# Three squares, a store's sum, four first products and the last column halves change places in a one-core attention and feed-forward kernel

## The chip, the cores and the metric

The kernel runs on one core of a Trainium2 chip. The metric is the device time of one execution in microseconds (us). Five executions of the kernel before are given; their median is 208.82 us. One more view of it is a profile: one execution recorded by the hardware, with the start and duration of every instruction, its span, and the landing of every transfer.

## What is computed

The reference has two steps. The first is a cross attention of tokens `x` (8 batches, 8 heads, 512 tokens, 64 columns) and 32 `state` rows per head, in both directions:

```
scores  = x @ state^T / 8          xread = softmax(scores)  @ state
scores2 = state @ x^T / 8          sread = softmax(scores2) @ x
a_out   = concat([xread, sread])   # 544 rows per head
```

The second takes the 8 batches x 544 rows of `a_out`, with the heads side by side as 512 columns, as tokens of a feed-forward layer with 2048 hidden units:

```
h = a_out @ w_in                   # 512 -> 2048
g = s * relu(h)^2 + b
out = g @ w_out                    # 2048 -> 512
```

`s` and `b` are scalars. The output has 4352 rows of 512 fp32 values.

## The kernel before, in words

**Stages of a batch.** For the 512 token rows of a batch, the kernel does not form `xread`. It multiplies the state with `w_in` first: `M` = state times `w_in` (`att_M`, four pieces of 512 hidden units, products into PSUM and a copy to SBUF), and then the hidden layer is `h = a4 @ M`, where `a4` are the softmax shares. The scores `T` (`att_T`) need `x` transposed (`xT`) and the state transposed (`stT`). For batches 0 and 1, `x` is transposed on TensorE (`att_xT_pe`), in two groups `g` of two PSUM tiles each, and the tiles are copied to SBUF, the second tile of a group by ScalarE, the first by VectorE; for later batches a DMA transposes. An exponential on ScalarE gives `E`. For batches 0 to 2 the shares come from sums by TensorE (`att_D`) with Ln and Exp on ScalarE and a product on VectorE; for batches 3 to 7 VectorE forms them in transposed layout (`att_shares`, tile `aT`) and a DMA transposes them into `a4` (`att_a4_dma`, line 307). `att_V` forms the read of the state rows, whose tokens of all batches are worked on at the end as "sr".

**Hidden layer.** `mm1_x(b, f)` forms 128 hidden units `f` (16 of them) of all 512 tokens with two products of 512 columns into a bank `h`. `mm1_close` takes the ReLU (ScalarE, for batch 0 and f = 1, 3, 5 VectorE) into a tile `r` of two `f`, in a pool of three buffers, and after every odd `f` squares the pair into `g` (line 428, VectorE). For batch 0 the squares of f = 1 and 3 are put into a list `held`, and worked off when the square of f = 5 comes.

**Second layer.** Most of it is done by a scheme with 7 block products instead of 8 (`fast_items`): p = 1 to 7, each over 8 blocks k of the hidden units, on sums of token blocks (`token_sum`, VectorE) and of weight blocks (`weight_sums`). Three accumulators in PSUM, A, B and C, carry partial sums from one p to the next; after each p, VectorE takes a sum out (`done`, `put`, `put_last`), and stores go out. A tile in PSUM that VectorE reads is written again only when it has been read. "0b" is the second half of batch 0's tokens, in this scheme with one block of 128 tokens instead of two; the first half of batch 0 goes straight (`mm2_part`, accumulators `o`). For batch 7, accumulator C is two tiles of 256 columns, `oC_0` and `oC_1`, in the pool `psO`; its last product, p = 3, is done for the second of them in two column halves of 128, the second of which begins when VectorE has read the first.

**Order of the work.** TensorE, SP and GpSimd run in the order in which the program is written; for VectorE and ScalarE a scheduler orders the instructions, and `tc.issue_after(i)` puts an instruction behind `i`. Within a batch s, the loop at line 953 runs over f; around each `mm1_x(s, f)` it puts the stages of batch s + 1 (`pieces`) and a slice `items[f]` of seven second-layer products, of batch s - 1 at first and of batch s in the last slices. For batches 2 to 6 the slice comes ahead of `mm1_x` where 4 <= f < 13, and behind it elsewhere (line 956). After batch 7 come the state rows and the rest of batch 7's second layer, in the order of the calls of `go` (lines 1014 to 1025).

Of the kernel before, what the change touches and what calls it, by code (L numbers as in the profile page):

```python
# [9 lines left out]
FP32 = mybir.dt.float32  # L10
# [4 lines left out]
def kernel(  # L15
# [10 lines left out]
    nc = tc.nc  # L26
    AF = mybir.ActivationFunctionType
    ALU = mybir.AluOpType
# [6 lines left out]
    P = 128  # L35
# [10 lines left out]
    NDT = 3  # L46
    NH = DM // 2
# [15 lines left out]
    psH = ctx.enter_context(tc.tile_pool(name="psH", bufs=2, space=bass.MemoryType.PSUM))  # L63
# [5 lines left out]
    def mm(out, lhsT, rhs, start=True, stop=True, tp=None, is_transpose=None):  # L69
        return nc.tensor.matmul(  # L70
            out,
            lhsT,
            rhs,
            start=start,
            stop=stop,
            tile_position=tp,
            is_transpose=is_transpose,
            skip_group_check=True,
        )
# [21 lines left out]
    s_bc = konst.tile([P, 1], FP32, name="s_bc")  # L101
# [75 lines left out]
    xT_done = {}  # L177
# [226 lines left out]

    held = []

    def mm1_close(key, hps, ntok, f):
        if f % 2 == 0:
            pool, tag, n = (apool, "ET", 3) if (key, f) == (0, 0) else (rpool, "r", 3)
            R2[key] = pool.tile([P, 2, ntok], FP16, name=f"r_{key}_{f}", tag=tag, bufs=n)  # L410
        r16 = R2[key]
        if key == 0 and f in (1, 3, 5):
            nc.vector.tensor_scalar(r16[:, f % 2], hps, 0.0, None, ALU.max)
            G["last"] = nc.cur_bb.bb.instructions[-1]
        else:
            nc.scalar.activation(r16[:, f % 2], hps, AF.Relu)  # L416
            G["relu"] = nc.cur_bb.bb.instructions[-1]
        if f % 4 == 0:
            G4[key, f // 4] = gpool.tile([P, 4, ntok], FP16, name=f"g_{key}_{f}", tag="g")
        gt = G4[key, f // 4]  # L420
        G[key, f] = gt[:, f % 4]
        if key == 1 and f in (3, 5):
            with tc.issue_after(nc.cur_bb.bb.instructions[-1]):
                nc.scalar.square(gt[:, f % 4 - 1 : f % 4 + 1], r16)
        elif f % 2 == 1:

            def square():
                nc.vector.tensor_mul(gt[:, f % 4 - 1 : f % 4 + 1], r16, r16)  # L428

            if key == 0 and f in (1, 3):  # L430
                held.append(square)
                return
            while held:
                with tc.issue_after(G["last"]):
                    held.pop(0)()
                G["last"] = nc.cur_bb.bb.instructions[-1]
            square()
            G["last"] = nc.cur_bb.bb.instructions[-1]

# [44 lines left out]
    def x_dst(b, rr):  # L484
        return out_BSn[b, 0:S].rearrange("(q c) n -> c q n", c=SCH)[chunk_of(rr)]
# [64 lines left out]
    def fast_items(b):  # L550
# [11 lines left out]
        def lhs(p, k, i):  # L562
            c = P * i
            a = c0 + c
            if p == 1:
                return G[key, k][:, a : a + P]
            if p == 2:
                return G[key, 8 + k][:, a : a + P]
            if p == 4:
                return G[key, 8 + k][:, th + a : th + a + P]  # L570
            si = {3: 4, 5: 1, 6: 2, 7: 3}[p]
            return SQ[b, si, k // 4][:, k % 4, c : c + P]

        def rhs(p, k):
            if p == 1:
                return wof(k)[:, 0:NH]
            if p == 2:
                return wof(8 + k)[:, 0:NH]
            if p == 3:
                return wof(8 + k)[:, NH:DM]  # L580
            ti = {4: 3, 5: 0, 6: 1, 7: 2}[p]
            return wd[ti][k // 4][:, k % 4, :]
# [9 lines left out]
        def put(bank, add, j, n0):  # L592
            if b == "sr":
                ends.append(own[1][:, len(ends) : len(ends) + 1])
                osb = ends[-1]
            elif j == 1:
                osb = add
            else:
                osb = opool.tile([P, ni, NH], FP32, name=f"osb_{b}_{j}_{n0}", tag="osb")
            if bank == "C" and b == last_b:  # L600
                for i in range(ni):
                    nc.vector.scalar_tensor_tensor(
                        osb[:, i], acc["C", i], s_bc, add[:, i], ALU.mult, ALU.add
                    )
            else:
                nc.vector.scalar_tensor_tensor(osb, acc[bank], s_bc, add, ALU.mult, ALU.add)
            if b == "sr":
                for i in range(4):
                    dst = out_BSn[4 * j + i, S:ST, n0 : n0 + NH]
                    eng = nc.sync if i % 2 else nc.scalar  # L610
                    eng.dma_start(dst, osb[Ns * i : Ns * i + Ns, 0])
                return
            if b == "0b":
                nc.gpsimd.dma_start(x_dst(0, 2 + j)[:, n0 : n0 + NH], osb[:, 0])
                return
            dst = out_BSn[b, 0:S].rearrange("(q ci cj) n -> cj q ci n", ci=2, cj=2)
            nc.gpsimd.dma_start(dst[j][:, :, n0 : n0 + NH], osb)  # L617

        def put_last(i, w=slice(0, NH)):
            ends.append(spare(f"osb_last_{len(ends)}"))  # L620
            osb = ends[-1][:, i, w]
            nc.vector.scalar_tensor_tensor(  # L622
                osb, acc["C", i][:, w], s_bc, kept["u2"][:, i, w], ALU.mult, ALU.add
            )
            dst = out_BSn[b, 0:S].rearrange("(q ci cj) n -> cj ci q n", ci=2, cj=2)
            dst = dst[0][i][:, NH:DM][:, w]
            if len(ends) == 1:
                nc.scalar.dma_start(dst, osb)
            elif len(ends) == 2:
                nc.sync.dma_start(dst, osb)  # L630
            else:
                for eng, p in ((nc.sync, 0), (nc.scalar, P // 2)):
                    eng.dma_start(dst[p : p + P // 2], osb[p : p + P // 2])
# [28 lines left out]
        def item(p, k, i, h=None):  # L662
            bank = {1: "A", 2: "A", 6: "B", 7: "B", 4: "B", 5: "C", 3: "C"}[p]
            fresh = p in (1, 6, 5) and k == 0
            if bank == "C" and b == last_b:
                if fresh:
                    acc[bank, i] = psO.tile([P, NH], FP32, tag="o", name=f"oC_{b}_{i}")
                dst = acc[bank, i]
            else:
                fresh = fresh and i == 0  # L670
                if fresh:
                    pool, tag = psO, "o"
                    if b == "sr":
                        pool, tag = (psH, "h") if bank == "C" else (psA, "att")
                    acc[bank] = pool.tile([P, ni, NH], FP32, tag=tag, name=f"o{bank}_{b}")
                dst = acc[bank][:, i, :]
            if h is not None:
                w = slice(P * h, P * h + P)
                mm(dst[:, w], lhs(p, k, i), rhs(p, k)[:, w], start=False, stop=(k == 7))
                if k == 7:  # L680
                    put_last(i, w)
                return
            mm(dst, lhs(p, k, i), rhs(p, k), start=fresh, stop=(k == 7))
            if p == 3 and b == last_b:
                if k == 7:
                    put_last(i)
            elif k == 7 and i == ni - 1:
                done(p)

# [6 lines left out]
            order = [(p, 0, 8) for p in (1, 6, 2, 7, 5, 4, 3)]  # L696
        out = [(p, k, i) for p, k0, k1 in order for k in range(k0, k1) for i in range(ni)]
        if b == last_b:
            out += [(5, k, i) for i in range(ni) for k in range(8)]
            out += [(3, k, 0) for k in range(8)]  # L700
            out += [(3, k, 1, h) for h in range(2) for k in range(8)]
        return [lambda a=a: item(*a) for a in out]

    def bias_sum():
# [53 lines left out]
    with tc.manual_schedule(engines={ET.PE, ET.SP, ET.Pool}):  # L758
# [67 lines left out]
        with tc.issue_after(A[0]["exp"]):  # L826
# [5 lines left out]
        warm_up(2)  # L832
        mm1_x4(0, 0, lambda: att_M(0, 1, "split"))

        b0 = {
            4: [lambda: att_M(0, 2, "split")],
            9: [lambda: att_xT_pe(1, 0), lambda: att_xT_pe(1, 1)],
            10: [lambda: att_T(1, [0, 1])],
            11: [
                lambda: att_M(0, 3, "split"),  # L840
# [95 lines left out]
        for s in range(1, B):  # L936
# [16 lines left out]
            for f in range(NKF):  # L953
                for fn in todo_s.get((f, "ahead"), []):
                    fn()
                if 1 < s < last_b and 4 <= f < 13:
                    for fn in items[f]:
                        fn()
                    items[f] = []
# [28 lines left out]
                    late_sum = sums.pop()  # L988
                for fn in items[f]:
                    fn()  # L990
                if s == 1 and f == 8:
                    with tc.issue_after(G["u2", "0b"]):
                        sums.pop(0)()
                    sums.append(late_sum)
# [7 lines left out]
        def go(items, n):  # L1002
            for _ in range(n):
                items.pop(0)()
# [15 lines left out]
                token_sum("sr", i, 1)  # L1020
        go(rest, 8)
        go(rows, 4)
        go(rest, 8)
        go(rows, 44)
        go(rest, len(rest))

# [28 lines left out]
```

## Time and profile before

| what | value |
|---|---|
| five executions, us | 208.69, 208.74, 208.82, 209.57, 209.67 |
| median, us | 208.82 |
| profiled execution, us | 209.57 |
| its span, us | 207.8 |
| TensorE matmul busy, share of the span | 198.3 us, 95% |
| VectorE busy | 166.1 us, 80% |
| ScalarE busy | 127.8 us, 62% |
| GpSimd busy | 38.8 us, 19% |
| bytes moved by DMA | 25.52 MB, mean 123 GB/s |
| TensorE clock granted | full, in all slices |

How to read the rows that follow. PE is TensorE's matmul side, PEld its weight loads, DVE is VectorE, ACT ScalarE, POOL GpSimd, SP the queue of SyncE. A row of the order of time gives the start in us, the busy time in us, engine, line, operation, output and inputs by the program's names, how many instructions are merged (x16), and in brackets how long the engine stood idle before them and what ended that. Matmuls are pipelined: the row of a matmul ends when its last result is out, while the next can start much earlier. A row of a wait gives who waited for whom, the total in us, how often, and the longest. "h", "oA", "oB", "oC", "T", "D" and "Mps" are PSUM tiles of the stages above; line 70 is the helper that issues every matmul.

### The profile page before, as it was taken

What the parts mean: (1) busy time and instruction counts of PE and PEld (TensorE: products, weight loads), DVE (VectorE), ACT (ScalarE), POOL (GpSimd) and SP (SyncE); (2) the same over time, 40 slices, a digit from 0 to 9 for tenths busy, and PEclk for the clock granted to TensorE, in tenths of its full rate; (3) what the DMA queues carried; (4) which work ended last, traced back from release to release, by engine and by line L of the source; (5) the groups of instructions that cost most, each with busy time, mean ns of one, the idle gap of its engine ahead of it and who ended that gap; (6) DMA issues with size and microseconds to landing.
All of it is one profiled execution on the core that took longest, in us unless ns stands there. A gap on an engine that the chain in (4) does not pass through costs nothing.

```text
span 207.8 us, 4884 instructions
## 1 busy us (share of the span) xinstructions
PE 198.3 (95%) x1978; PEld 133.1 (64%) x1978; DVE 166.1 (80%) x300; ACT 127.8 (62%) x253; POOL 38.8 (19%) x66
## 2 busy tenths in 40 slices
PE   7888999999999999999999899999999999999991
PEld 2424343566766776767666667676767777888891
DVE  4489679987969996899679966997699786796861
ACT  2578876899477657766676568675867545543100
POOL 5870002413210231023102101120112012100210
PEclk9999999999999999999999999999999999999999
DMA  5999996999999495939891924160416011300243
GB/s 170 229 201 206 207 192 102 183 196 160 138 193 180 117 182 73 201 87 205 126 101 56 194 66 104 50 161 0 101 54 158 3 50 50 106 0 2 89 129 90
DMA packets 46795, 25.52 MB, mean 123 GB/s; under 512 B 31604, under 2 KB 44788, under 8 KB 46772
## 3 DMA queue, kind: packets, MB, share of 16 engines
q0 software_dynamic: 15568, 16.19, 40.0%
q1 hardware_dynamic: 30324, 8.52, 25.3%
q10 hardware_dynamic: 880, 0.49, 0.9%
q8 instruction: 15, 0.25, 0.5%
q14 instruction: 8, 0.07, 0.1%
HBM read 17.30 MB, written 8.91 MB: 126 GB/s over the span
## 4 chain that ended last, share of the span: by engine, by line
PE 85%; DVE 5%; DMA 4%; ACT 3%; issue 1%; POOL 0%; DVEq 0%
PE h L70 24%; PE oB L70 18%; PE oC L70 12%; PE oA L70 11%; PE Mps L70 4%; PE o L70 3%; PE h_sr L70 3%; DMA a<-aT 2%; DMA stf<-in_state_dram 2%; DVE g L428 2%; PE V L70 1%; PE oB_sr L70 1%; PE T L70 1%; ACT r L416 1%; DVE M L337 1%
## 5 line engine op out<-in xcount | busy, mean ns | idle before, releaser
L416 ACT ACTIVATE r<-h 128x512 f16<-128x512 f32 x125 | 73.9, 602 | 44.9 <-PE h L70 44.3
L70 PE MATMUL h<-a,M 128*128 128x512 f16 x256 | 74.1, 379 | 1.1 <-DMA a<-aT 0.6
L70 PEld LDWEIGHTS <-s 128*128 128x128 f16 x456 | 44.0, 98 | 16.3 <-issue 0.6
L428 DVE TENSOR_TENSOR g<-r 128x1024 f16<-128x1024 f16 x62 | 42.0, 683 | 13.6 <-ACT r L416 13.1
L70 PEld LDWEIGHTS <-g 128*128 128x128 f16 x392 | 37.3, 98 | 18.5 <-issue 4.4
L70 PE MATMUL oB<-wd,s 128*128 128x256 f16 x224 | 32.8, 273 | 0.0
L70 PE MATMUL oA<-wo,g 128*128 128x256 f16 x224 | 32.5, 273 | 0.0
L70 PEld LDWEIGHTS <-M 128*128 128x128 f16 x256 | 24.4, 98 | 11.6 <-issue 2.2
L617 POOL DMA_DIRECT2D out_dram<-osb x13 | 8.8, 674 | 70.5 <-DVE rt L352 36.2
L314 ACT CAST M<-Mps 128x1024 f16<-128x1024 f32 x20 | 20.1, 1007 | 0.0
L70 PE MATMUL oC<-wd,s 128*128 128x256 f16 x112 | 16.5, 273 | 0.0
L70 PE MATMUL oC<-wo,s 128*128 128x256 f16 (+1 forms) x120 | 15.5, 265 | 0.4 <-DVE osb_last L622 0.4
L70 PE MATMUL oB<-wd,g 128*128 128x256 f16 x112 | 15.7, 273 | 0.0
L617 POOL DMA_DIRECT2D out_dram<-u x7 | 4.7, 678 | 41.7 <-DVE inv L297 27.5
L416 ACT ACTIVATE r_sr<-h_sr 128x256 f16<-128x256 f32 x16 | 6.1, 382 | 7.9 <-PE h_sr L70 6.4
L644 DVE SCALAR_TENSOR_TENSOR u<-oB,s_bc,qa 128x512 f32<-128x512 f32 x7 | 5.2, 750 | 6.4 <-PE oB L70 6.2
L238 ACT ACTIVATE E<-T 128x256 f16<-128x256 f32 x20 | 7.4, 383 | 4.0 <-PE T L70 4.0
L546 DVE TENSOR_TENSOR s<-s,g 128x1024 f16<-128x1024 f16 x14 | 9.6, 687 | 0.2
L70 PE MATMUL h_sr<-srdT,wi 128*128 128x256 f16 x64 | 9.6, 273 | 0.0
L548 DVE TENSOR_TENSOR s<-g,s 128x1024 f16<-128x1024 f16 x14 | 9.6, 685 | 0.0
L544 DVE TENSOR_TENSOR s<-g,g 128x1024 f16<-128x1024 f16 x14 | 9.6, 684 | 0.0
L539 DVE TENSOR_TENSOR s<-g 128x1024 f16<-128x1024 f16 x14 | 9.5, 686 | 0.0
(137 smaller groups left out, 242.3 us busy)
## 6 DMA issues: line engine op xcount, KB each, us to landing
out_dram<-osb POOLq DMA_DIRECT2D x15, 256.0 KB, 4.4
xn<-in_x_dram POOLq DMA_DIRECT2D x7, 512.0 KB, 9.4
wi<-in_moe_w_in_dram POOLq DMA_DIRECT2D x4, 512.0 KB, 9.0
wo<-in_moe_w_out_dram POOLq DMA_DIRECT2D x4, 512.0 KB, 16.1
out_dram<-u POOLq DMA_DIRECT2D x7, 256.0 KB, 2.5
out_dram<-qb POOLq DMA_DIRECT2D x7, 256.0 KB, 3.2
xf<-in_x_dram SPq DMA_DIRECT2D x2, 512.0 KB, 5.2
out_dram<-osb_0b POOLq DMA_DIRECT2D x2, 128.0 KB, 6.4
```

Of the source, the lines that this page charges most:

```text
L70: return nc.tensor.matmul(out, lhsT, rhs, start=start, stop=stop, tile_position=tp, is_transpose=is_transpose, skip_group_check=True,)
L238: nc.scalar.activation(a["E"][:, g, 256 * m : 256 * m + 256], Ts[m][:, g, :], AF.Exp, scale=scale, accum_out=a["rs"][:, NG * m + g : NG * ...
L314: nc.scalar.copy(dst, ps)
L337: nc.vector.tensor_copy(dst[:, 0], two[0])
L416: nc.scalar.activation(r16[:, f % 2], hps, AF.Relu)
L428: nc.vector.tensor_mul(gt[:, f % 4 - 1 : f % 4 + 1], r16, r16)
L539: nc.vector.tensor_sub(o, a11, a21)
L544: nc.vector.tensor_add(o, a21, a22)
L546: nc.vector.tensor_sub(o, SQ[b, 1, j], a11)
L548: nc.vector.tensor_sub(o, a12, SQ[b, 2, j])
L617: nc.gpsimd.dma_start(dst[j][:, :, n0 : n0 + NH], osb)
L644: nc.vector.scalar_tensor_tensor(u, acc["B"], s_bc, kept["qa"], ALU.mult, ALU.add)
```

## The change

Four places are changed.

1. In batch 0 the squares of f = 1, 3, 7 and 9 are held. The square of f = 3 is released ahead of that of f = 5. Those of f = 1, 7 and 9 are released behind VectorE's last copy of batch 1's transposed tokens.
2. The square of batch 1, f = 11, is held and put behind the sum that is taken out of oC of "0b" in that step.
3. For batches 3 to 6 (`NDT` is 3), the slice of seven products of f = 0 comes ahead of the first products of the hidden layer.
4. For batch 7 the second tile of accumulator C is two tiles of 128 columns, the first in the pool `psO`, the second in `psH`, in product p = 5 already; p = 5 of this tile is thus 16 products of 128 columns where it was 8 of 256, and the sum behind it is two instructions.

```diff
+    def release(i, n):
+        for _ in range(n):
+            with tc.issue_after(G["last"]):
+                held.pop(i)()
+            G["last"] = nc.cur_bb.bb.instructions[-1]
...
-            if key == 0 and f in (1, 3):
+            if (key, f) in ((0, 1), (0, 3), (0, 7), (0, 9), (1, 11)):
                 held.append(square)
                 return
-            while held:
-                with tc.issue_after(G["last"]):
-                    held.pop(0)()
-                G["last"] = nc.cur_bb.bb.instructions[-1]
+            if (key, f) == (0, 5):
+                release(1, 1)
             square()
...
             if bank == "C" and b == last_b:
-                for i in range(ni):
+                for o, i, w in [
+                    (acc["C", 0], 0, slice(0, NH)),
+                    (acc["C", 1, 0], 1, slice(0, P)),
+                    (acc["C", 1, 1], 1, slice(P, NH)),
+                ]:
                     nc.vector.scalar_tensor_tensor(
-                        osb[:, i], acc["C", i], s_bc, add[:, i], ALU.mult, ALU.add
+                        osb[:, i, w], o, s_bc, add[:, i, w], ALU.mult, ALU.add
                     )
...
             if b == "0b":
+                G["put", b] = nc.cur_bb.bb.instructions[-1]
                 nc.gpsimd.dma_start(x_dst(0, 2 + j)[:, n0 : n0 + NH], osb[:, 0])
...
+            if h is not None:
+                if fresh:
+                    pool, tag = (psH, "h") if h else (psO, "o")
+                    acc[bank, 1, h] = pool.tile([P, P], FP32, tag=tag, name=f"oC_{b}_1_{h}")
+                w = slice(P * h, P * h + P)
+                mm(acc[bank, 1, h], lhs(p, k, i), rhs(p, k)[:, w], start=fresh, stop=(k == 7))
+                if k == 7:
+                    if p == 3:
+                        put_last(acc[bank, 1, h], i, w)
+                    elif h == 1:
+                        done(p)
+                return
...
-            out += [(5, k, i) for i in range(ni) for k in range(8)]
-            out += [(3, k, 0) for k in range(8)]
-            out += [(3, k, 1, h) for h in range(2) for k in range(8)]
+            for p in (5, 3):
+                out += [(p, k, 0) for k in range(8)]
+                out += [(p, k, 1, h) for h in range(2) for k in range(8)]
...
+        def behind_xT():
+            G["last"] = xT_done[1, 1, 0]
+            release(0, 3)
...
-            9: [lambda: att_xT_pe(1, 0), lambda: att_xT_pe(1, 1)],
+            9: [lambda: att_xT_pe(1, 0), lambda: att_xT_pe(1, 1), behind_xT],
...
-                if 1 < s < last_b and 4 <= f < 13:
+                if 1 < s < last_b and (4 <= f < 13 or (f == 0 and s >= NDT)):
                     for fn in items[f]:
                         fn()
                     items[f] = []
...
                 for fn in items[f]:
                     fn()
+                if s == 1 and f == 11:
+                    G["last"] = G["put", "0b"]
+                    release(0, 1)
...
-        go(rest, 8)
+        go(rest, 16)
         go(rows, 44)
         go(rest, len(rest))
```

## The prediction

> **What bounds the kernel now.** I read the page first, then who waited for whom on TensorE, then the order of time around each of those waits, and last the single records inside them.
>
> ```profile
> PE 198.3 (95%) x1978; PEld 133.1 (64%) x1978; DVE 166.1 (80%) x300; ACT 127.8 (62%) x253; POOL 38.8 (19%) x66
> ...
> PE 85%; DVE 5%; DMA 4%; ACT 3%; issue 1%; POOL 0%; DVEq 0%
> ```
>
> PE is busy for 95% of the span, and the chain that ended last lies on it for 85%. From 24 us to 203 us its single records follow one another at the pitch of their size (0.109 us for 256 columns, 0.216 for 512), so a microsecond taken from the middle of the kernel comes only from a place where PE stands still. The waits on TensorE's own rows name few:
>
> ```profile
> PE T L70 <- DVE xT L200: 1.0, 1, 1.0
> ...
> PE h L70 <- DMA a<-aT: 0.6, 1, 0.6
> ...
> PE oC L70 <- DVE osb_last L622: 0.4, 1, 0.4
> PE oC_0b L70 <- DVE u_0b L606: 0.3, 1, 0.3
> ```
>
> These columns count from the modelled end of the matmul before. Measured from start to start against the pitch, the same four holes are larger: 1.12 (and 0.33 just after it), 0.74, 0.61 and 0.50 us. The edits sit on exactly these four places.
>
> The profiled execution took 209.57 us, its span 207.80; 1.77 lie around it. The five runs shown are 208.69, 208.74, 208.82 and 209.57, 209.67. The third hole, 0.74, is about the distance between the two groups, so I read the median 208.82 as an execution in which that transfer was in time, and the profiled one as one in which it was late.
>
> **Part 1: batch 1's copies ahead of three squares.** In order of time, first PE, then VectorE and ScalarE:
>
> ```profile
> 18.11 1.06 PE L70 MATMUL xTps<-ident,xn 128*128 128x128 f16 x16
> 19.31 0.59 PE L70 MATMUL h<-a,M 128*128 128x512 f16 x2
> 20.86 0.76 PE L70 MATMUL T<-xT,stT 64*32 64x256 f16 x16 [0.96 <-DVE xT L200]
> 21.55 0.60 PE L70 MATMUL h<-a,M 128*128 128x512 f16 x2
> ```
>
> ```profile
> 17.28 3.19 DVE L428 TENSOR_TENSOR g<-r 128x1024 f16<-128x1024 f16 x5
> ...
> 18.66 1.08 ACT L416 ACTIVATE r<-h 128x512 f16<-128x512 f32 x2 [0.56 <-DVE g L428]
> ...
> 20.39 0.75 DVE L200 COPY xT<-xTps 128x512 f16<-128x512 f16 x2
> ```
>
> The transposes are done at 19.17, but VectorE works off five squares (starts 17.28, 17.88, 18.48, 19.08, 19.78) and copies at 20.39 and 20.72, until 21.14. PE's T products wait for that. After the change VectorE's order is: square of f=3, of f=5, the two copies, then the squares of f=1, 7, 9. Nothing is added, five instructions change places. VectorE is free at 18.48, the first four transposes end at 18.28 + 0.22 = 18.50, the third four at 18.95, so the copies (0.42 each) end near 18.99 and 19.43. Now ScalarE sets it. Its ReLU of f=8 needs the r buffer that the square of f=3 gives back; that square is now first and ends at 17.96 instead of 18.56, so the ReLU starts 0.10 after it, at 18.06 instead of 18.66; two ReLUs at 0.49, then ScalarE's two copies start at 19.03 and 19.50 and the last (0.62) ends at 20.12. The h products of f=10, which waited for that ReLU (19.31), run at 19.01. The last copy that T needs is thus at 20.12, not 21.14: 1.02. Less of T is then left (6 products, not 14, whose 0.36 to the next h shrinks by up to 0.1). Gain 1.02 to 1.12; I take 1.05. What follows (exponentials, D, the copies of M, h of f=12) hangs from T and from h of f=11 and comes forward with them. The three squares put behind the copies run from 19.4 to 21.25 and are hidden: the next VectorE work, the copy of M, has its products only at 22.50 - 1.07 = 21.43. Were they 0.3 later, M would be late by about 0.1.
>
> What could hold the gain back are loads that don't come forward. By the landings in the trace, the fourth piece of w_in lands at 20.70 and its first use moves from 22.09 to 21.04: 0.34 of slack. The first two pieces of w_out land at 22.83 and 25.41, their uses move to 23.5 and 26.5. If w_in's piece were 0.5 later in other executions, 0.2 of the gain would go.
>
> **Part 2: the square of batch 1, f=11, behind a store's sum.**
>
> ```profile
> 47.21 0.69 DVE L428 TENSOR_TENSOR g<-r 128x1024 f16<-128x1024 f16 x1 [0.65 <-ACT r L416]
> 47.82 0.16 DVE L353 RECIPROCAL rq<-rs 128x2 f32<-128x2 f32 x1
> 47.90 0.46 DVE L606 SCALAR_TENSOR_TENSOR u_0b<-oC_0b,s_bc,u_0b 128x256 f32<-128x256 f32 x1
> ```
>
> ```profile
> 48.41 0.27 PE L70 MATMUL oC_0b<-wo,s_0b 128*128 128x256 f16 x1 [0.34 <-DVE u_0b L606]
> ```
>
> PE wants to go on in the bank of oC_0b at 47.91 and gets it at 48.41, when u_0b has been read out: 0.50. u_0b stands behind a square that waits until 47.21 for ScalarE, though its own products ended near 46.34. After the change only the reciprocal is ahead of it (ScalarE's accumulators, 46.69), so it runs at about 46.85 to 47.31, 0.60 before PE comes. The square then runs at 47.31 to 48.0 and the next sum (48.28 before) at 48.1. Gain 0.50. Behind it, ScalarE is in arrears here (no idle from 45.4 to 51.9), so PE comes nearer to it: V needs a bank that Ln leaves at 48.58 and comes at 48.88, 0.30 to spare; the token sum that oB of batch 1 needs keeps some 0.5. I take 0.50, bounds 0.2 and 0.5.
>
> **Part 3: first products of batches 3 to 6 behind seven others.** Each of four batches moves 2 products of 0.216 behind 7 of 0.109; no count changes, and no DMA or queue is passed.
>
> ```profile
> 116.21 0.93 PE L70 MATMUL oA<-wo,g 128*128 128x256 f16 x7
> 117.72 0.61 PE L70 MATMUL h<-a,M 128*128 128x512 f16 x2 [0.58 <-DMA a<-aT]
> ```
>
> In batch 5 the transposed shares landed at 117.67 (issued 113.01) where PE was ready at 116.98. The seven products take 0.76, so h would be due at 117.74: the hole of 0.74 closes, by a hair. In batches 3, 4 and 6 there is no hole, nor in 5 in the shorter executions by my reading: gain 0.74 for an execution like the profiled one, 0 for the median. Price: the seven come 0.43 earlier and need a token sum, which VectorE ends at 74.19 for a use at 74.78 (batch 3) and 116.67 for 116.98 (batch 5), and a bank that is read out 0.6 earlier still. That holds with 0.3 to 0.6. The ReLU of f=0 moves 0.76 later; h of f=2 needs its bank and still comes 0.4 after it. I cost it at 0; if a sum were 0.3 late, each batch would pay 0.3.
>
> **Part 4: the last column halves in own banks.**
>
> ```profile
> 202.48 0.80 DVE L622 SCALAR_TENSOR_TENSOR osb_last<-oC,s_bc,u 128x256 f32<-128x256 f32 x2 [0.39 <-PE oC L70]
> ...
> 203.33 0.61 PE L70 MATMUL oC<-wo,s 128*128 128x128 f16 x8 [0.44 <-DVE osb_last L622]
> ...
> 203.97 0.35 DVE L622 SCALAR_TENSOR_TENSOR osb_last<-oC,s_bc,u 128x128 f32<-128x128 f32 x1 [0.70 <-PE oC L70]
> ...
> 204.36 0.58 ACTq L633 DMA_DIRECT2D out_dram<-osb_last  x1
> ```
>
> The last eight products start 0.66 after their forerunner where 0.056 is the pitch: 0.605 saved, since they no longer share a tile with what VectorE reads. The price is product 5's second half in 16 narrow products instead of 8 wide ones. By this kernel's own rows that is 16 x 0.056 - 8 x 0.109 = +0.02. The Trainium skill speaks against the split: "TensorE: Matmul & The Clock Gate", section "Back-to-back issue gap", has some 81 ns per product of 128 columns in a stream that loads weights each time, not 56. By that it would be 16 x 0.081 - 0.872 = +0.42, and the gain of this part only 0.1. The row is the same stream (each with its own weight load, at 202.28 to 202.67), so I take the row. VectorE gets one sum more: two of 0.35 for one of 0.48, about 0.17 more by their starts. Behind them is the sum that PE waits for at 197.91; it now ends near 197.89, plus 0.05: 0 to 0.2 lost, I take 0.04. The last sum moves from 203.97 to about 203.42; SP and ACT are free from the stores before at 203.66 and 203.60. Those stores (192 KB) landed at 205.12 and 205.40, the last at 206.64; coming nearer to them, the last may lose up to 0.3. I take 0.50 for the part, bounds 0.1 and 0.6.
>
> **The sum.** For the profiled execution 1.05 + 0.50 + 0.74 + 0.50 = 2.79: 209.57 - 2.79 = 206.8. For the median, without part 3, 2.05: 208.82 - 2.05 = 206.8.
>
> **The rivals.**
> *Loads take part 1's place* (0.15). w_in's fourth piece, or w_out's, comes later in most executions than in this one, and PE meets it. For: the slack is 0.34, and the loads are slow and queued (9.0 us from issue to landing for w_in, 16.1 for w_out, by the page's medians). Against: the queue before it is the same. Up to all of 1.05 goes: 207.3 to 207.8.
> *The tail keeps its end* (0.12). The last stores wait behind the 192 KB, or the narrow products cost what the page states: part 4 gives 0.1, so 207.2.
> *A new wait at the head of batches 3 to 6* (0.07), the other side. PE asks 0.43 earlier for the token sum (line 546 before the change) and its bank, ahead of h, and ScalarE's and VectorE's chain of the batch starts 0.76 later. It decides when four waits exceed 2.05, which is 0.51 a batch; above 0.67 the kernel is over 0.3% slower. VectorE would have to be 1 us later than in the trace. Then near 209.8.
> *The change doesn't do what it says* (0.06). The copies still wait for ScalarE, which is now the later one, or another load ahead fills the holes; 208.5 to 209.
>
> **How the numbers follow.** The likeliest case, 206.8, has 0.60, and its own range is 206.4 to 207.2. The measurement tells 0.3%, 0.63 us, from no change. The range takes in the bounds of part 1 and part 4 below (206.4) and the first two rivals above: 206.3 to 207.8. It leaves out the last two rivals (0.13) and some edges. Faster: 0.60 + 0.15 + 0.12 and a third of the last, 0.89; within 0.3%: 0.04; slower: 0.07.
>
> **What would show it.** Right: T starts near 19.5 and h of f=11 near 20.5; no wait of oC_0b for u_0b; D near 22.0; no wait of h for the shares, or one under 0.1; the last products without a hole, and the last sum 0.5 after the one before it (1.05 now). Wrong: a TensorE wait on w_in or w_out before 27 us; on a token sum or the oC read-out at the first oB of a batch; a last store over 2.6 us from issue to landing.

## The result and the profile after

Against the kernel before, timed beside it, the changed kernel takes 0.9918 of the time, 95% interval 0.9892 to 0.9944: 207.1 us from the median of 208.82. Set beside the kernel before once more (e9) it took 0.9959, 0.9931 to 0.9986. These ratios leave out executions over 1.5% above the fastest of their kernel, and here that hides a part of the effect: the middle of all executions is 209.93 against 209.10 in the first series, and 208.64 against 208.65 in the second. Of the executions whose clock is on record, 24 of 50 of the changed kernel show a mean granted TensorE clock of 0.992 or less (1 is the full clock), and 3 of 143 of the kernel before. The runs below show that this comes with the change.

The profiled execution took 207.87 us, its span is 206.1 (209.57 and 207.8 before). The waits of TensorE in it, longest first:

```profile
PE T L70 <- DMA xT<-xn: 1.2, 1, 1.2
...
PE Mps L70 <- DMA wi<-in_moe_w_in_dram: 0.3, 1, 0.3
...
PE T L70 <- ACT xT L200: 0.2, 1, 0.2
```

All four waits of before are gone: T for VectorE's copy, h for the shares, oC_0b for u_0b, and the last oC. At their head stands a new one, T for a transposed `x`. In order of time on TensorE, at the places of the four parts:

```profile
18.83 0.43 PE L70 MATMUL T<-xT,stT 64*32 64x256 f16 x10
19.46 0.40 PE L70 MATMUL T<-xT,stT 64*32 64x256 f16 x6 [0.21 <-ACT xT L200]
...
20.67 0.62 PE L70 MATMUL Mps<-wi,stT 64*32 64x512 f16 x16 [0.27 <-DMA wi<-in_moe_w_in_dram]
...
46.53 0.27 PE L70 MATMUL oC_0b<-wo,s_0b 128*128 128x256 f16 x1
...
56.23 0.41 PE L70 MATMUL Mps<-wi,stT 64*32 64x512 f16 x8
57.89 0.44 PE L70 MATMUL T<-xT,stT 64*32 64x256 f16 x16 [1.25 <-DMA xT<-xn]
...
116.54 0.93 PE L70 MATMUL oB<-wd,s 128*128 128x256 f16 x7
117.31 1.03 PE L70 MATMUL h<-a,M 128*128 128x512 f16 x4
...
200.23 1.93 PE L70 MATMUL oC<-wo,s 128*128 128x256 f16 x24
```

Batch 1's T now waits for ScalarE's last copy, with six products left, as forecast; M's products then wait for w_in. oC_0b and the last 24 products of oC run on without a hole, h of batch 5 no longer waits. Ahead of T of batch 3, at 57.89, TensorE stands still for 1.25 us. Since TensorE is the bound, the time between two of its records tells what a stretch gained or lost. From both traces, in us:

| stretch, by TensorE's records | before | after | difference |
|---|---|---|---|
| start to batch 1's transposes | 18.11 | 17.41 | -0.70 |
| to the first product of o (part 1) | 6.45 | 5.77 | -0.69 |
| to V of batch 0 (part 2) | 24.82 | 24.33 | -0.49 |
| to T of batch 3 | 8.95 | 10.38 | +1.43 |
| to V of batch 4 | 50.56 | 50.57 | +0.01 |
| to V of batch 5 (part 3) | 21.85 | 21.10 | -0.75 |
| to oC of the state rows | 68.04 | 68.06 | +0.02 |
| to the last product (part 4) | 4.93 | 4.33 | -0.60 |
| to the end of the span | 4.08 | 4.15 | +0.07 |

The sum is -1.71, which is the difference of the spans. The first row is nothing that the change does: it is 17.0 to 17.9 in all twelve experiments, whichever kernel they are. It goes with the clock at the start, which is not full in all slices, though the table of the profile before has it so: in the profile of before the first record of the full clock is at 7.12 us, and the products ahead of it follow one another at 0.427 us for 512 columns, twice the later pitch; after the change it is at 3.87. The three traces in which it comes latest (6.9 to 7.1 us) are the three that reach batch 1's transposes latest (17.8 to 18.1). The fourth row takes back more than half of what the parts give. Its cause stands on two queues. GpSimd's and SP's rows, first before:

```profile
48.66 0.54 POOL L614 DMA_DIRECT2D out_dram<-u_0b  x1 [4.23 <-DVE u_0b L606]
49.19 0.92 POOL L121 DMA_DIRECT2D xn<-in_x_dram  x1
```

```profile
46.58 3.17 SPq L208 DMA_TRANSPOSE xT<-xn  x1
```

and after:

```profile
46.20 0.54 POOL L623 DMA_DIRECT2D out_dram<-u_0b  x1 [3.16 <-DVE u_0b L614]
46.73 0.91 POOL L121 DMA_DIRECT2D xn<-in_x_dram  x1
```

```profile
47.34 5.30 SPq L208 DMA_TRANSPOSE xT<-xn  x1
```

The load of x for batch 4 stands on GpSimd behind the store of u_0b, and this store waits for VectorE's sum. The earlier start and parts 1 and 2 bring both forward by 2.46 us. The transposing DMA of batch 3 doesn't come forward: it starts when x3 has landed (46.4 to 48.3 in all fourteen traces), and that load is issued at 39.0 to 40.3 in all of them, when batch 2's transposed `x` has landed, so it hangs on a chain of transfers and not on TensorE. So a load that had begun 2.6 us behind the transposing DMA now begins 0.6 ahead of it. The DMA lands 10.5 us after its issue instead of 5.7, at 57.84, where T had been ready at 56.45. This late landing and the hole behind it are called the fault below; a hole is counted from one start to the next, less the pitch, which gives 1.43 here.

### The profile page after: what moved, and what is told of

It is laid out like the page before. It is cut to its first block, busy times and chain, and to the rows that moved or that the text cites. A ratio compares the mean times of both kernels' runs of the same rounds, so it can differ in the third digit from the quotient of the medians.

```text
span 206.1 us, 4900 instructions
## 1 busy us (share of the span) xinstructions
PE 196.9 (96%) x1986; PEld 132.8 (64%) x1986; DVE 165.8 (80%) x301; ACT 127.4 (62%) x253; POOL 38.7 (19%) x66
## 4 chain that ended last, share of the span: by engine, by line
PE 82%; DMA 13%; POOL 1%; DVE 1%; SPq 0%; issue 0%
PE h L70 23%; PE oB L70 17%; PE oC L70 12%; PE oA L70 11%; DMA wi<-in_moe_w_in_dram 6%; DMA xT<-xn 5%; PE Mps L70 4%; PE o L70 4%; PE h_sr L70 3%; DMA xf<-in_x_dram 3%; PE oB_0b L70 1%; PE oB_sr L70 1%; PE V L70 1%; PE oA_sr L70 1%; PE oC_sr L70 1%; PE oA_0b L70 1%
## 5 line engine op out<-in xcount | busy, mean ns | idle before, releaser
L70 PE MATMUL oC<-wd,s 128*128 128x256 f16 (+1 forms) x120 | 16.5, 266 | 0.0
```

Of the source, the lines that this page charges most:

```text
L70: return nc.tensor.matmul(out, lhsT, rhs, start=start, stop=stop, tile_position=tp, is_transpose=is_transpose, skip_group_check=True,)
```

## The experiments

Theory 1 is that chain: earlier sum, earlier store, earlier load of x4, late transposing DMA, hole at T of batch 3, and in a long hole a lower clock. Theory 2 is that the long executions come from elsewhere. Each time below is the middle (the median) of all executions, against that of the kernel before on the same chip; the ratios are formed as above.

**e1: the load of x4 held back.** To the change, this is added:

```diff
+        def gated_x4():
+            nc.gpsimd.tensor_copy(gate, A[3]["xT"][0:1, 0, 0, 0:1])
+            load_x(4)
...
-                at(12, lambda: load_x(4))
+                at(12, gated_x4)
```

> All four parts of the change, and the load of x for batch 4 held back on GpSimd until batch 3's transposed x has landed. Theory 1 (the load of x4, brought forward by part 2 and started beside the transposing DMA of batch 3, makes that DMA late, and T of batch 3 stops TensorE, 1.4 us in the trace, long enough in other executions to bring the clock down): the wait of T for the transposed x is gone, the DMA is issued in about 3 us and not 5.3, executions with a granted clock under 0.993 go away or get rare, and the time is about 2.5 us under that of the kernel before. Theory 2 (the long executions and their lower clock come from elsewhere, for example from the first 25 us): as many long executions with a clock near 0.992 as with the change alone, and a gain of no more than 1.7 us in the others.

Measured: 206.68 against 208.70, ratio 0.9898 (0.9856 to 0.9940). The DMA is issued in 2.9 us and lands 4.8 after, at 51.59; T has no hole. One of 6 executions is at 0.992, and it is at 207.13. That is what theory 1 expects, 0.5 short of its 2.5.

**e2 and e3: part 2 taken out, and part 2 alone.** The diff is that of e2, against the change; in e3 the kernel before gets part 2 by lines that do the same.

```diff
-            if (key, f) in ((0, 1), (0, 3), (0, 7), (0, 9), (1, 11)):
+            if (key, f) in ((0, 1), (0, 3), (0, 7), (0, 9)):
...
-                if s == 1 and f == 11:
-                    G["last"] = G["put", "0b"]
-                    release(0, 1)
```

> The change without its part 2: the square of batch 1, f=11, stays where it was. Theory 1: the store of u_0b and the load of x4 behind it start after the transposing DMA of batch 3 (by about 1 us), T of batch 3 waits little or not at all, long executions get rare; 1.5 us under the kernel before, that is no worse than the whole change although a gain of 0.5 is given up. Theory 2: as many long executions as with the whole change, and the others 0.5 us slower than those of it.

> Part 2 alone. The hole of 0.50 us at oC_0b is gone. Theory 1: the load of x4 comes some 0.8 to 1.3 us earlier against the transposing DMA of batch 3, which is then slower than 3.2 us to issue; T of batch 3 is asked for at 57.8 and waits little or not at all: 0.5 us under the kernel before, or less where the DMA is late. Theory 2: 0.5 us under the kernel before in all executions.

Measured: e2 208.12, ratio 0.9944 (0.9916 to 0.9972), 4 of 22 executions at 0.992; e3 209.25, 0.9991 (0.9957 to 1.0025), 3 of 14 at 0.992 or less. Both miss what I expected of T: its hole is 1.81 us in e2 and 2.55 in e3. In e2 the load starts 0.44 us behind the transposing DMA, in e3 0.08 ahead, and either is near enough. So part 2 alone brings the fault about (e3), and its 0.50, which the trace has in full, can't be told from nothing in the time; without part 2 the fault is not gone (e2). That part 1 brings it about by itself is not shown: in e2's trace the load begins at 48.14, as in that of e4, which has neither part, and it is the transposing DMA that starts later (47.70 against 46.67). How near the two come thus depends on the execution as well.

**e4: part 4 alone.** The diff is the change's own for accumulator C, with the other three parts undone.

> Part 4 alone. By my sum 0.50 us under the kernel before (bounds 0.1 and 0.6), by the trace of the change rather 0.6: the last 16 narrow products without a hole, the last store landed about 2.3 us after its issue. If the narrow products cost 81 ns each or the last stores queue, 0.1 us. Neither theory on the long executions expects any here beyond those of the kernel before.

Measured: 208.00 against 208.70, 0.9973 (0.9952 to 0.9993). The stretch to the last product is 0.60 shorter, the stretch behind it 0.02 longer. Two rows, TensorE and VectorE:

```profile
200.22 1.93 PE L70 MATMUL oC<-wo,s 128*128 128x256 f16 x24
```

```profile
201.29 1.24 DVE L631 SCALAR_TENSOR_TENSOR osb_last<-oC,s_bc,u 128x256 f32<-128x256 f32 x3 [0.39 <-PE oC L70]
```

The three last sums now follow one another. The narrow products keep 0.056 us each: the stretch that holds product 5 lengthens by 0.02, not 0.42. The 81 ns of the expectation are the figure of the Trainium skill that the prediction cites ("TensorE: Matmul & The Clock Gate", "Back-to-back issue gap"); this stream doesn't show it.

**e5 and e6: the suspected cause alone, and its cure alone, on the kernel before.** In e5 GpSimd waits for x3 and then loads x4; in e6 it waits for the transposed x of batch 3, as in e1.

```diff
+        def x4_at_x3():
+            nc.gpsimd.tensor_copy(gate, xn[3][0:1, 0, 0, 0:1])
+            load_x(4)
...
-                at(12, lambda: load_x(4))
+                at(10, x4_at_x3)
```

> The kernel before, without any part of the change, with the load of x4 issued at the moment when x3 has landed, that is beside the transposing DMA of batch 3. Theory 1: this alone makes the fault: the transposed x lands 10 to 12 us after its issue and not 5.7, T of batch 3 (asked for at 57 to 58 us) waits 0.5 to 2.8 us, executions with a granted clock near 0.992 are common, the middle of all executions is 1 to 2 us above that of the kernel before. Theory 2 (the long executions come with the change's other moves on VectorE and TensorE): nothing but the kernel before, within 0.3 us.

> The kernel before, with the load of x4 held back until batch 3's transposed x has landed, and nothing else. Theory 1: the fault is in some of the executions of the kernel before too (those above 209 us), so they go away: the fastest stay at 207.9 to 208.2, the middle of all falls by about 0.4 us. If the gain of the first experiment came from the hold alone and not from the change, it is 2 us under the kernel before.

Measured: e5 209.47 against 208.94, ratio 1.0008 (0.9981 to 1.0036); the DMA lands 12.1 us after its issue and T's hole is 0.92. From the SyncE queue and the waits of TensorE in e5:

```profile
46.86 3.01 SPq L208 DMA_TRANSPOSE xT<-xn  x1
```

```profile
PE T L70 <- DMA xT<-xn: 0.7, 1, 0.7
```

The fault is made by the load alone. Its cost at the kernel before's pace is not resolved: 0.5 at the middle, nothing in the ratio, less than I expected, and none of 22 executions is at 0.992. e6: 209.01, ratio 0.9999 (0.9973 to 1.0025). Its highest of 14 is 209.87, where 7 of 49 of the kernel before lie above 210, which 14 executions can't settle, and the middle did not fall as I expected. So the hold has no worth of its own that these times show: what e1 gains is the change's.

**e7 and e8: e1 without part 3, and without part 1.** The first diff is e7's, the second e8's.

```diff
-                if 1 < s < last_b and (4 <= f < 13 or (f == 0 and s >= NDT)):
+                if 1 < s < last_b and 4 <= f < 13:
```

```diff
-            if (key, f) in ((0, 1), (0, 3), (0, 7), (0, 9), (1, 11)):
+            if (key, f) in ((0, 1), (0, 3), (1, 11)):
...
-                release(1, 1)
+                release(0, 2)
...
-            9: [lambda: att_xT_pe(1, 0), lambda: att_xT_pe(1, 1), behind_xT],
+            9: [lambda: att_xT_pe(1, 0), lambda: att_xT_pe(1, 1)],
```

> The first experiment (the change with the load of x4 held back) without part 3. If part 3 is worth nothing in executions in which batch 5's shares are in time, the fastest are as fast as there (205.9), and some are 0.6 to 0.9 slower, where the shares land late; the middle of all 0.2 to 0.7 above the first experiment. If part 3 costs something at the head of batches 3 to 6, it is faster than the first experiment.

> The first experiment without part 1. By my sum 1.05 us slower than it; where the last piece of w_in lands after TensorE asks for it (0.34 and 0.87 us of wait in two traces of part 1), 0.3 to 0.8 slower.

Measured: e7 207.01 against 208.94, ratio 0.9900 (0.9870 to 0.9930); e8 207.42, 0.9936 (0.9911 to 0.9960). e1 and its repetition are 2.0 and 2.3 under the kernel before, e7 is 1.9 and e8 1.5. By the middles part 1 is thus worth 0.5 to 0.8, but the intervals of e8 and e1 overlap. Part 3's worth can't be told from nothing in the time; in the traces it is plain. From the waits of TensorE in e7:

```profile
PE oC L70 <- DVE u L614: 0.6, 1, 0.6
...
PE h L70 <- DMA a<-aT: 0.4, 1, 0.4
```

The second is the hole at the head of batch 5, 0.60 by the pitch. The first is another one, where the DMA that transposes E comes late to VectorE; e5 has it too, 0.98 by the pitch. It is in some traces and not in others, so it may be one reason why the times of a kernel spread over more than part 3 can give.

**e9 to e12: the change, the hold, a simpler order, and the load beside the DMA.** e9 is the change and e10 is e1. e11 has no wait, only another place in GpSimd's order:

```diff
-                at(12, lambda: load_x(4))
...
             if s == 2:
+                at(1, lambda: load_x(4))
                 at(1, lambda: load_x(5))
```

e12 is the change with the edit of e5.

> The change as it stands, once more, on the chip of the runs beside it. By theory 1 T of batch 3 waits 1 to 3 us for the transposed x; where the hole is near 2.7 us or longer the clock falls for one window (0.992). The middle of all executions is above that of the kernel before, the undisturbed ones 1.5 us under it.

> The first experiment once more, to set it against the change on one chip: no wait of T of batch 3, no or few executions at 0.992, 2.0 us under the kernel before.

> The change with the load of x4 put one place later in GpSimd's own order, behind the store of osb_0b and directly ahead of the load of x5, with no wait for the transposed x. It should be issued near 51 us, some 4 us after the transposing DMA of batch 3 and not 0.6 before it. Theory 1: that suffices, as in the hold: T of batch 3 doesn't wait, 2.0 us under the kernel before. If only the wait itself matters (the two transfers must not touch at all), part of the stall stays.

> The change with the load of x4 issued when x3 has landed, beside the transposing DMA of batch 3 in every execution. T of batch 3 is asked for near 56.3 and the DMA lands near 58 to 59: a hole of 1.5 to 3 us. If long holes bring the clock down, more than half of the executions show 0.992 or less, and the middle of all is 1 to 3 us above the kernel before; if the clock has another cause, their share is what the kernel before shows (some 1 in 25).

Measured, with 208.65 for the kernel before: e9 208.64 and 0.9959 (0.9931 to 0.9986), 9 of 22 executions at 0.992 or less; e10 206.31 and 0.9895 (0.9851 to 0.9939); e11 206.27 and 0.9883 (0.9849 to 0.9917), none of 6 below 0.996; e12 208.09 and 0.9952 (0.9933 to 0.9971), 2 of 22 at 0.992. e9's middle is level with the kernel before, not above it as I expected, and its 13 executions at a higher clock have their middle at 207.63, 1.0 under it and not 1.5. The intervals of e9 and e11 don't touch: e11 beats the change as well as the kernel before. With the load of x4 held back or moved (e1, e7, e8, e10, e11), 2 of 44 executions are at 0.992 or less. GpSimd's, SP's and TensorE's rows of e11:

```profile
45.92 0.54 POOL L623 DMA_DIRECT2D out_dram<-u_0b  x1 [3.16 <-DVE u_0b L614]
47.23 0.54 POOL L623 DMA_DIRECT2D out_dram<-qb_0b  x1 [0.77 <-DVE qb_0b L614]
50.62 0.54 POOL L623 DMA_DIRECT2D out_dram<-osb_0b  x1 [2.85 <-DVE osb_0b L614]
51.15 1.82 POOL L121 DMA_DIRECT2D xn<-in_x_dram  x2
```

```profile
47.02 3.75 SPq L208 DMA_TRANSPOSE xT<-xn  x1
```

```profile
55.94 0.41 PE L70 MATMUL Mps<-wi,stT 64*32 64x512 f16 x8
56.17 0.40 PE L70 MATMUL T<-xT,stT 64*32 64x256 f16 x16
```

The load is 4.1 us behind the transposing DMA, which lands after 6.4 us, at 53.40. The two still overlap somewhat, and T doesn't wait: they need not be kept apart wholly.

The profile of e9 fell on an execution with the lower clock. Its stretches on all engines; the clock stands behind "POOL busy":

```profile
core 0: us, PE busy (x) PEld busy (x) DVE busy (x) ACT busy (x) POOL busy (x), PEclk, DMA share, GB/s
53.50:56.20 2.70, 2.70 (x23) 1.91 (x20) 2.56 (x5) 1.50 (x3) 0.00 (x0) 1.00 1.23 210
56.20:60.59 4.39, 1.91 (x42) 1.10 (x41) 1.89 (x4) 0.91 (x6) 0.00 (x0) 1.00 1.42 178
60.59:64.01 3.42, 3.42 (x14) 1.77 (x13) 0.87 (x3) 2.20 (x7) 0.68 (x1) 0.50 0.79 106
64.01:67.50 3.49, 3.49 (x27) 2.41 (x25) 2.76 (x5) 2.55 (x4) 0.00 (x0) 1.00 1.14 241
```

Behind the hole (T waits 2.48 us there, until 59.15) half the clock is granted for 3.41 us, in which products of 256 columns follow one another at 0.213 us and not 0.109; the stretch from there to V of batch 1 is 1.69 longer than before. e3 shows the same behind its hole, half a clock from 59.79 to 63.20, 1.58 longer. Half of 3.41 us is 0.8% of the span, so a mean clock of 0.992 is the size of one such fall. Only these two were traced, and e1's execution at 0.992 was not long. All traces on one row each, by how far the load of x4 is issued behind the transposing DMA:

| kernel | load behind DMA, us | issue to landing, us | hole at T, us | clock falls |
|---|---|---|---|---|
| e9, the change | -0.74 | 11.6 | 2.67 | yes |
| the change | -0.61 | 10.5 | 1.43 | no |
| e3 | -0.08 | 12.1 | 2.55 | yes |
| e2 | +0.44 | 11.4 | 1.81 | no |
| e12 | +0.48 | 10.8 | 1.80 | no |
| e5 | +0.48 | 12.1 | 0.92 | no |
| e4 | +1.47 | 9.6 | 0 | no |
| before | +2.61 | 5.7 | 0 | no |
| e11 | +4.13 | 6.4 | 0 | no |
| e8, e6, e1, e10, e7 | +5.0 to +5.9 | 4.4 to 5.2 | 0 | no |

e12 missed its expectation of long holes and low clocks. A load half a us behind the DMA makes a hole of 1.8, as in e2; the holes of 2.5 and over are in two of the three traces in which the load is ahead of the DMA. Why the order of the two weighs so much, if it does, is open. That the clock fell so seldom in e12 fits what the last section finds. e4, at +1.47, has no hole by only 1.0 us.

## Why the prediction was right or wrong, point by point

**The number** was right: 206.8 forecast, 207.1 measured, inside 206.3 to 207.8, and faster. That is in part luck. Of the 1.71 between the two profiles, 0.70 is the earlier start, which is not the change's; the parts give some 2.4, and the hole that I did not foresee takes 1.43 back. The repetition's ratio of 0.9959 would be 208.0, outside the range, and the middle of all executions shows no gain in either series. Without the fault (e1, e10, e11) the gain is 2.0 to 2.4, where the parts were put at 2.05.

**The step that failed is in part 2**, "Behind it, ScalarE is in arrears here ... I take 0.50, bounds 0.2 and 0.5". Its 0.50 is right to the hundredth: 0.49 to 0.50 in all nine traces that have it. What it left out is the queue that the moved sum feeds. I followed u_0b to TensorE's bank and to the banks behind it, not to the store on GpSimd and the load of x4 behind the store. What the runs showed in its place: the load of x4 comes 2.46 us earlier, runs beside the transposing DMA of batch 3, and this DMA lands after 10.5 us instead of 5.7. The second place is part 1, "loads that don't come forward": I asked for w_in and w_out alone. The load of x3 and its transposing DMA don't come forward either, and T of batch 3 asks for them 1.9 us earlier. With the 5.7 us of before it would have landed at 53.0, 3.4 us ahead of T, so the earlier use alone would have cost nothing; only the collision does. None of my rivals was this one.

**Part 1** was put at 1.05. It measured 0.69 in the profile, 0.31 to 1.06 in the eight traces that have it, against the stretch of before, 6.45, which is 6.45 or 6.46 in four of the five others without part 1 and 6.22 in e4. The term that was mis-sized is the slack of w_in's last piece, which I took as 0.34 from one execution and costed at 0. The piece lands at 20.2 to 20.9 in all traces, but TensorE reaches batch 1's transposes at 17.2 to 17.9 in these eight where the profile of before has 18.1, so it asks for the piece at 20.0 to 20.7, not at the 21.04 that I had forecast, and in seven of them waits for it. Where the transposes begin at 17.86 (e10) the gain is 1.06; at 17.35 with the piece at 20.91 (e2) it is 0.31. So the first rival came true in part, though what I held against it is right too: the loads come much as before, and it is TensorE that comes earlier.

**Part 3** closes the hole of 0.74, and in the eight traces with it h of batch 5 never waits for the shares. That it gives nothing to the median was wrong by the traces: the six kernels without it that were traced have holes of 0.74, 0.14, 0.58, 0.67, 0.48 and 0.60, so I was wrong to read the gap between two groups of five times as this hole being there or not. In the time it wasn't resolved. The new wait at the head of batches 3 to 6, the rival on the other side, is in no trace.

**Part 4** gave 0.60 less 0.02 and up to 0.07 at the end, 0.5 to 0.6 where I took 0.50. The narrow products and VectorE's additional sum cost 0.02 together (0.02 and 0.04 forecast). The skill's 81 ns for a narrow product with its own weight load was refused by the rows: 0.056, before and after. The rival in which the last stores wait behind others fell: the stretch from the last product to the end is 4.08 before and 3.9 to 4.15 with part 4.

## What to carry to other kernels

When an instruction is moved forward, follow everything that its result releases, stores and the loads behind them on their queue too, and ask what other transfer will now run beside them. Loads that hang from the start of the kernel don't come forward with the compute; list each use that does, with its slack in more than one execution. A wait of TensorE can cost more than its length (in e9 a hole of 2.67 us cost 1.69 more through the clock), so look at the granted clock of every execution and not only of the profiled one.

## What the runs showed of the hardware

A transposing DMA of SP with a 512 KB load from GpSimd's queue beginning within 0.8 us of it lands after 10.5 to 12.1 us. With the load 1.5 us behind it lands after 9.6 (e4), 2.6 behind after 5.7, and 4 us or more behind after 4.4 to 6.4. By the packets of the trace after the change SP's queue is slower while GpSimd's is busy: from 51 to 54 us SP's queue starts 197 packets per us beside 192 of GpSimd's, and from 54 to 56, beside 44 of GpSimd's, 672. What sets these shares isn't shown.

The clock goes down and up on a fixed grid. In e9 it is first granted in full at 5.98 us, falls 54.613 us later (16 times 3.4133), and comes back after 3.413. In e3 it falls 54.613 after its first grant at 5.18. In the other twelve traces it falls only at the end, 197.973 or 201.386 us after the first grant (58 and 59 times 3.4133). Whether it falls goes with how long TensorE was busy within one window of this grid. The windows that end in the two falls, e9's and e3's, and one of e12's, at the end of which it stayed full (columns as above):

```profile
57.18:60.59 3.41, 1.44 (x32) 0.98 (x33) 0.91 (x3) 0.91 (x5) 0.00 (x0) 1.00 1.45 179
```

```profile
56.37:59.79 3.42, 1.06 (x34) 0.38 (x32) 1.75 (x3) 0.06 (x2) 0.00 (x0) 1.00 1.53 143
```

```profile
56.27:59.68 3.41, 1.79 (x40) 1.04 (x37) 1.77 (x4) 0.96 (x5) 0.00 (x0) 1.00 1.40 149
```

Counted over all fourteen traces, the grid has 820 windows at the full clock. The 16 that end in a fall, 14 of them at the end of the kernel, were busy for 0 to 1.44 us, and the 804 others for 1.80 or more. So a hole need not fill a window: one of 2.55 us brought the clock down in e3, and one of 1.8 just did not in e2 and e12. Where between 1.44 and 1.80 the limit lies, and what the chip itself counts as busy, these traces don't show. The Trainium skill, "TensorE: Matmul & The Clock Gate", section "What's actually happening", states the free-running window of 3413 ns and the half rate, which these traces show (the first grant lies at 3.87 to 7.12 us); its table has the low rate follow an idle window, and here windows that were busy for 31% and 42% of their length sufficed.
